# Streaming attention and a wave layer on one core: the order of all steps from a list schedule, and the values of both head parities in one two-bank tile

## The chip, the cores and the metric

The kernel runs on one core of a Trainium2 chip. TensorE (PE) multiplies matrices and writes to PSUM, VectorE (DVE), ScalarE (ACT) and GpSimd (POOL) do the rest, and transfers are issued from the queues of SyncE (SP) and POOL. Each engine takes its instructions in the order in which the program wrote them. The metric is device time in microseconds of one execution, as the median of several runs.

## The reference, cut to what matters

```python
# q, k, v: 4 batches x 8 heads x 768 positions x 64; heads 0, 2 and 6 are "retrieval"
scores = scale * np.matmul(q, k.transpose(0, 1, 3, 2))
stream_keep = causal & (is_sink | in_win)      # 4 sink keys, or a window of 64
mask = np.where(retr, causal, stream_keep)
a = softmax(np.where(mask, scores, -1e9))
x = np.matmul(a, v)                            # heads side by side: 4 x 768 x 512
theta = x @ w_theta
zr, zi = x * np.cos(theta), x * np.sin(theta)
y = w_tok_r @ zr + w_tok_i @ zi                # over the 768 positions
u = x + y
return u + np.maximum(u @ w_ch, 0.0)
```

## The kernel before, in words

Heads are taken in four pairs, n = 0 to 3, and positions in blocks of 128. For each batch b the steps are these. `transposes(b, n)` turns q and k of a pair (PE, line 151) and copies them out of PSUM (ACT line 155, DVE line 157). `score_unit` multiplies keys by queries (line 215) into a two-bank tile `ps`, ACT takes the exponential (lines 231 to 243), and DVE multiplies a causal triangle (lines 253, 256) or the window mask (line 224) in; there are 14 such units a batch and one for the sink keys (line 283). `cast_v` makes bf16 values `vt` and a copy `vx` shifted by half a block. `values(b, i)` multiplies probabilities by values for one block i (line 312), first for the even heads and then for the odd, each in a one-bank tile `pav`; DVE takes a reciprocal (line 314) and multiplies (line 316). `turn_x` turns x, `phases` multiplies by w_theta (line 333), ACT takes cosine and sine (lines 338, 339), DVE makes zr (line 341) and POOL zi (line 342). `mix` multiplies by the two token weights (line 372), adds x (line 376), turns u (line 353), multiplies by w_ch (line 360), makes the output tile `ot` (line 362) and stores it. Token weights are turned on the chip too (line 393). Three pools hold PSUM: `ps_s` has two tiles of two banks (scores, phases), `ps_m` two of one bank (mix, channel) and `ps_x` two of one bank (all transposes and `pav`).

The order is what the program writes. Generators yield at places with an estimated cost in ns, and `weave` always continues the one that is least far along its given total; it runs attention of batch b + 1 beside `mix` of batch b. Within attention, the order is a list written by hand. The first batch stands ahead of this, written out:

```python
    weave((scores(high_all, 7, 1), 6300), (early(0), 5500))
```

The transfers of weights and of the next q and k are issued from POOL's queue at places in the same text; v and the output go through SP's queue.

Of the kernel before, what the change touches and what calls it, by code (L numbers as in the profile page):

```python
# [9 lines left out]
F32 = mybir.dt.float32  # L10
# [11 lines left out]
def drain(gen):  # L22
    for _ in gen:
        pass


def weave(*parts):

    live = [[0.0, n, g, float(total)] for n, (g, total) in enumerate(parts)]
    while live:  # L30
        live.sort(key=lambda x: (x[0] / x[3], x[1]))
        part = live[0]
        try:
            part[0] += next(part[2])
        except StopIteration:
            live.pop(0)
# [3 lines left out]
def kernel(  # L40
# [17 lines left out]
    NB = S // 128  # L58
    KD = DM // 128
# [19 lines left out]
    m_causal = const.tile([128, 128], BF16, name="m_causal")  # L79
# [9 lines left out]
    kS = [big.tile([128, 128], BF16, name=f"kS{n}") for n in range(4)]  # L89
# [8 lines left out]
    NQ = S // 64  # L98
    P_st = big.tile([128, len(STREAM), NQ * 128 + 64], BF16, name="P_st")

    state = {}


    def load_v(b, pairs=range(4), after=None):
        src = v[b].rearrange("h (j p) d -> p h j d", p=128)
        for n in pairs:
            t = stage.tile([128, 2, NB, D], F32, tag="st_v", name="st_v")
            state["v", b, n] = t
            if after is not None:

                nc.vector.tensor_copy(t[:, :, 0, 0], after[:, :2])
            for x, h in enumerate(PAIRS[n]):
                nc.sync.dma_start(out=t[:, x], in_=src[:, h])


    def load_qk(b, heads=slice(0, 8)):
        for what, a in (("q", q), ("k", k)):
            if (what, b) not in state:
                state[what, b] = two.tile([128, H, NB * D], BF16, tag=f"{what}b", name=f"{what}b")
            src = a[b].rearrange("h (p j) d -> p h (j d)", p=128)  # L120
            nc.gpsimd.dma_start(out=state[what, b][:, heads], in_=src[:, heads])

    def cast_v(b, n, first=False):
        t = state["v", b, n]
        h0, h1 = PAIRS[n]
        (nc.vector if first else nc.gpsimd).tensor_copy(vt[:, h0:h1 + 1:2, :, :D], t)  # L126
        for x, h in enumerate((h0, h1)):
            if not IS_RETR[h]:
                s = STREAM.index(h)
                if first:  # L130
                    nc.vector.tensor_copy(vx[:64, s], vt[:64, h])  # L131
                    nc.vector.tensor_copy(vx[64:, s, 1:], vt[64:, h, :NB - 1])
                else:
                    nc.gpsimd.tensor_copy(vx[:64, s, :, :D], t[:64, x])
                    nc.gpsimd.tensor_copy(vx[64:, s, 1:, :D], t[64:, x, :NB - 1])

    def sinks(n):
# [7 lines left out]
    def transposes(b, n):  # L145
        h0, h1 = PAIRS[n]
        for what, dst in (("q", qT), ("k", kT)):
            pt = ps_x.tile([128, 1024], BF16, tag="x", name="pt")
            for j in range(NB):
                for x, h in enumerate((h0, h1)):  # L150
                    nc.tensor.transpose(pt[64 * x:64 * x + 64, j * 128:(j + 1) * 128], state[what, b][:, h, j * D:(j + 1) * D], ident)  # L151
            o = dst[n].rearrange("d (p j) -> d p j", j=NB)
            i = pt[:, :S].rearrange("d (j p) -> d p j", j=NB)
            if (what == "q" and n < 2) or (b > 0 and (what == "q" or n < 2)):
                nc.scalar.copy(o, i)  # L155
            else:
                nc.vector.tensor_copy(o, i)
        sinks(n)
# [16 lines left out]
    pending = []  # L175

    def masks_now():
        while pending:
            pending.pop(0)()

    def score_unit(n, banks, un):
        ps = ps_s.tile([128, 2, 512], F32, tag="s", name="ps")
# [3 lines left out]
        if used:  # L186
            P = big.tile([128, sum(used)], BF16, tag=f"P{un}", name=f"P{un}")
        masks = []
        for y, (x, h, what) in enumerate(banks):
            rows = slice(64 * x, 64 * x + 64)  # L190
            if isinstance(what, list):
                c = 0
                for j, q0, w in what:
                    mms[y].append((ps[:, y, c:c + w], kT[n][rows, j * 128:(j + 1) * 128], qT[n][rows, q0:q0 + w]))
                    for i in range(q0 // 128, (q0 + w) // 128):
                        at = y * used[0] + c + i * 128 - q0
                        state["P", h, j, i] = P[:, at:at + 128]
                        if i == j:
                            masks.append(at)
                    c += w  # L200
                width.append(c)
            else:
                q0, w = what
                for c in range(NQ):
                    lo = max(64 * c if c != 1 else 0, q0)
                    hi = min(64 * c + 128, S, q0 + w)
                    if lo < hi:
                        half = slice(64 * (c % 2), 64 * (c % 2) + 64)
                        mms[y].append((ps[half, y, lo - q0:hi - q0], kT[n][rows, c * 64:(c + 1) * 64], qT[n][rows, lo:hi]))
                width.append(w)  # L210
        for m in range(max(map(len, mms))):
            for y in range(2):
                if m < len(mms[y]):
                    o, l, r = mms[y][m]
                    nc.tensor.matmul(o, l, r, start=True, stop=True, skip_group_check=True)  # L215
# [6 lines left out]
        def stream_mask(o, q0, w, heads):  # L222
            m = m_stream[:, q0:q0 + w].rearrange("p (c x) -> p c x", x=64).unsqueeze(1).to_broadcast([128, heads, w // 64, 64])
            nc.vector.tensor_tensor(o, o, m, ALU.mult)

        lists = [isinstance(what, list) for _, _, what in banks]
        w0, w1 = width
        if not any(lists):
            q0, w = banks[0][2]
            o = stream_out(banks[0][1], 2, q0, w)  # L230
            nc.scalar.activation(o, ps[:, :, :w].rearrange("p s (c x) -> p s c x", x=64), AF.Exp, scale=scale)  # L231
            pending.append(lambda: stream_mask(o, q0, w, 2))
        elif all(lists):
            if w0 == w1:
                nc.scalar.activation(P.rearrange("p (y c) -> p y c", y=2), ps[:, :, :w0], AF.Exp, scale=scale)  # L235
            else:
                assert w0 == 512
                nc.scalar.activation(P, ps.rearrange("p y c -> p (y c)")[:, :512 + w1], AF.Exp, scale=scale)
        else:
            nc.scalar.activation(P, ps[:, 0, :w0], AF.Exp, scale=scale)  # L240
            q0, w = banks[1][2]
            o = stream_out(banks[1][1], 1, q0, w)
            nc.scalar.activation(o[:, 0], ps[:, 1, :w].rearrange("p (c x) -> p c x", x=64), AF.Exp, scale=scale)
            pending.append(lambda: stream_mask(o, q0, w, 1))

        def causal():
            todo = list(masks)
            while todo:
                at = todo.pop(0)
                if len(set(used)) == 1 and at + used[0] in todo:  # L250
# [330 lines left out]
```

## Time and profile before

| | |
|---|---|
| median of 3 runs | 257.67 us (254.26 to 260.39) |
| the profiled execution | 255.57 us, of which the span is 253.9 us |
| busy: PE, DVE, ACT, POOL | 196.1, 141.2, 115.8, 81.9 us |

The span is the time from the first to the last instruction; an execution's own time has 1.7 us more around it. A busy PE includes the modelled end of each matmul, so it isn't a PE at its peak; what counts is where PE sits idle, and until when.

### The profile page before, as it was taken

To read this page: it belongs to the slowest core of one execution; us is meant where nothing else is said; L and a number is where in the kernel's file an instruction comes from. 1 tells how busy PE (TensorE), PEld (TensorE's weight loads), DVE (VectorE), ACT (ScalarE), POOL (GpSimd) and SP (SyncE) were. 2 spreads that over 40 slices of the span, in tenths; PEclk is the share of its full clock that TensorE was granted. 3 is DMA by queue.
4 is the path that set the end of the run, shared out by engine and by line. 5 is a ranking of instruction groups with operands and counts; after the bars stand their busy time and mean duration, and the time that the engine had idled before them with its cause. 6 is when DMAs were issued, how large, how long until landed. Compare 5 with 4: busy or idle time off the path is not lost.

```text
span 253.9 us, 5096 instructions
## 1 busy us (share of the span) xinstructions
PE 196.1 (77%) x2124; PEld 111.2 (44%) x2124; DVE 141.2 (56%) x318; ACT 115.8 (46%) x150; POOL 81.9 (32%) x121
## 2 busy tenths in 40 slices
PE   1585004978668998896969999986699999959992
PEld 0452002765245455564424556543245665424440
DVE  6665106665824656763469477625584776572442
ACT  2435001544548892226698633355887332711110
POOL 8805000001952960003099700044593000650000
PEclk9999999999999999999999999999999999999998
DMA  5999990820056089901205597101100111021113
GB/s 77 179 198 218 193 205 10 186 65 3 0 96 114 5 182 180 235 28 41 85 1 125 112 196 153 41 3 60 65 3 0 44 45 41 0 83 44 50 74 124
DMA packets 39758, 22.62 MB, mean 89 GB/s; under 512 B 25912, under 2 KB 36664, under 8 KB 39736
## 3 DMA queue, kind: packets, MB, share of 16 engines
q0 software_dynamic: 11072, 9.70, 24.7%
q1 hardware_dynamic: 28664, 12.61, 19.2%
q8 instruction: 16, 0.26, 0.4%
q14 instruction: 6, 0.05, 0.1%
HBM read 25.71 MB, written 6.29 MB: 126 GB/s over the span
## 4 chain that ended last, share of the span: by engine, by line
PE 53%; ACT 14%; DMA 13%; DVE 8%; issue 5%; POOL 4%; SPq 1%; POOLq 0%; DVEq 0%; ACTq 0%
PE py L372 20%; DMA st_v<-in_v_dram 9%; PE pav L312 8%; PE ps L333 6%; PE pc L360 6%; PE ps L215 6%; ACT P L235 3%; DMA qb<-in_q_dram 3%; POOL zi L342 3%; ACT qT L155 3%; ACT st L339 2%; DVE ot L362 2%; ACT ct L338 2%; PE pt L151 2%; PE pt L353 2%
## 5 line engine op out<-in xcount | busy, mean ns | idle before, releaser
L342 POOL TENSOR_TENSOR zi<-x,st 128x512 bf16<-128x512 bf16 x24 | 30.9, 1306 | 123.0 <-ACT st L339 122.7
L372 PE MATMUL py<-zr,wtokTr 128*128 128x512 bf16 x144 | 39.4, 380 | 2.5 <-DVE zr L341 2.5
L372 PE MATMUL py<-zi,wtokTi 128*128 128x512 bf16 x144 | 39.2, 379 | 0.4 <-POOL zi L342 0.4
L235 ACT ACTIVATE P<-ps 128x1024 bf16<-128x1024 f32 (+2 forms) x24 | 21.1, 917 | 24.9 <-PE ps L215 24.9
L341 DVE TENSOR_TENSOR zr<-x,ct 128x512 bf16<-128x512 bf16 x24 | 20.9, 910 | 17.1 <-ACT ct L338 17.1
L215 PE MATMUL ps<-qT,kT 64*64 64x128 bf16 (+6 forms) x380 | 26.3, 263 | 5.1 <-ACT P L235 4.7
L312 PE MATMUL pav<-vx,P_st 128*128 128x65 bf16 x120 | 17.0, 201 | 16.4 <-DVE vx L131 16.4
L355 ACT COPY uT<-pt 128x512 bf16<-128x512 bf16 x24 | 14.2, 593 | 33.7 <-PE pt L353 33.7
L376 DVE TENSOR_TENSOR u<-x,py 128x512 bf16<-128x512 bf16 x24 | 16.5, 686 | 21.0 <-PE py L372 20.7
L360 PE MATMUL pc<-w_ch_sb,uT 128*128 128x512 bf16 x96 | 24.6, 380 | 2.8 <-DVE ot L362 2.8
L338 ACT ACTIVATE ct<-ps,half_pi 128x1024 f32<-128x1024 f32 x12 | 13.4, 1117 | 28.2 <-PE ps L333 27.2
L333 PE MATMUL ps<-w_theta_sb,xT 128*128 128x512 bf16 x96 | 23.3, 379 | 0.0
L312 PEld LDWEIGHTS <-P_st 128*128 128x128 bf16 x240 | 14.1, 103 | 20.7 <-issue 19.5
L362 DVE SCALAR_TENSOR_TENSOR ot<-pc,u 128x512 f32<-128x512 f32 x24 | 16.5, 689 | 11.5 <-PE pc L360 8.9
L215 PEld LDWEIGHTS <-kT 64*64 64x64 bf16 (+1 forms) x380 | 12.7, 111 | 20.5 <-issue 18.2
L316 DVE TENSOR_TENSOR x<-pav,r 128x256 bf16<-128x256 f32 x48 | 20.4, 424 | 1.7
L372 PEld LDWEIGHTS <-wtokTi 128*128 128x128 bf16 x144 | 13.0, 98 | 14.9 <-issue 3.3
L312 PE MATMUL pav<-vt,P 128*128 128x65 bf16 x252 | 15.6, 203 | 3.7 <-DVE vt L126 1.7
L231 ACT ACTIVATE P_st<-ps 128x1024 bf16<-128x1024 f32 (+1 forms) x16 | 12.9, 814 | 10.2 <-PE ps L215 10.2
L314 DVE RECIPROCAL r<-pav 128x4 f32<-128x4 f32 x48 | 8.6, 179 | 15.6 <-PE pav L312 15.0
L312 PE MATMUL pav<-vt,P_st 128*128 128x65 bf16 x120 | 17.2, 202 | 0.0
L372 PEld LDWEIGHTS <-wtokTr 128*128 128x128 bf16 x144 | 12.0, 97 | 11.8 <-issue 1.7
(75 smaller groups left out, 320.2 us busy)
## 6 DMA issues: line engine op xcount, KB each, us to landing
st_v<-in_v_dram SPq DMA_DIRECT2D x32, 192.0 KB
out_dram<-ot SPq DMA_DIRECT2D x24, 256.0 KB
qb<-in_q_dram POOLq DMA_DIRECT2D x3, 768.0 KB, 10.5
kb<-in_k_dram POOLq DMA_DIRECT2D x3, 768.0 KB, 14.6
wtok<-in_moe_w_tok_r_dram POOLq DMA_DIRECT2D x3, 384.0 KB, 10.2
wtok<-in_moe_w_tok_i_dram POOLq DMA_DIRECT2D x3, 384.0 KB, 11.8
w_theta_sb<-in_moe_w_theta_dram POOLq DMA_DIRECT2D x1, 512.0 KB, 11.0
w_ch_sb<-in_moe_w_ch_dram POOLq DMA_DIRECT2D x1, 512.0 KB, 8.6
```

The lines of the kernel that those rows point to most:

```text
L215: nc.tensor.matmul(o, l, r, start=True, stop=True, skip_group_check=True)
L235: nc.scalar.activation(P.rearrange("p (y c) -> p y c", y=2), ps[:, :, :w0], AF.Exp, scale=scale)
L312: nc.tensor.matmul(o, l, r, start=(m == 0), stop=True, skip_group_check=True)
L316: nc.vector.tensor_tensor(dst, av[:, :, :D], r.unsqueeze(2).to_broadcast([128, 4, D]), ALU.mult)
L333: nc.tensor.matmul(ps[:, y], xT[:, kk, (i + y) * 128:(i + y + 1) * 128], w_theta_sb[:, kk], start=(kk == 0), stop=(kk == KD - 1))
L338: nc.scalar.activation(ct, ps, AF.Sin, bias=half_pi)
L341: nc.vector.tensor_tensor(state["zr", b][:, i + y], x[:, i + y], ct[:, y], ALU.mult)
L342: nc.gpsimd.tensor_tensor(state["zi", b][:, i + y], x[:, i + y], st[:, y], ALU.mult)
L360: nc.tensor.matmul(pc, uT[t][:, kk], w_ch_sb[:, kk], start=(kk == 0), stop=(kk == KD - 1))
L362: nc.vector.scalar_tensor_tensor(ot, pc, 0.0, u[t], ALU.max, ALU.add)
L372: nc.tensor.matmul(py, w[:, s, t * 128:(t + 1) * 128], z[:, s], start=(n == 0), stop=(n == len(order) - 1))
L376: nc.vector.tensor_tensor(u[t], x[:, t], py, ALU.add)
```

## The change

All work becomes `Step`s with an engine, a duration in ns, the steps that must come first, a PSUM or SBUF slot that it takes and steps whose slots it gives back. `Plan.order` runs a list schedule over them: whenever an engine is free it takes the ready step with the longest remaining path, with penalties for a switch of TensorE's tile shape or of ACT's table, and the steps are then emitted in the order of their planned starts. The transfers are steps of a made-up engine "DMA", one after another. The weights' transfers get a `hold`: they are planned behind the cast of the third pair of v.

Beside the order, the change does these things. One two-bank tile from `ps_s` holds the values of both parities, with one reciprocal and one multiplication. The causal triangles move from DVE to POOL, as selects in place. The shifted copies `vx` of batch 0 and some clearing move from DVE to POOL, four of the six zi of batch 0 from POOL to DVE, and batch 0's copies of turned x from DVE to ACT. All 14 score units of batch 0 come ahead of its values.

```diff
+    LATENCY = {"PE": (230, 0), "ACT": (190, 60), "DVE": (120, 60), "POOL": (150, 60), "SP": (50, 0), "DMA": (2000, 0)}
+    SWITCH = {"PE": 95, "ACT": 1300}
+    HOLD = {"PE": 1500, "ACT": 8000}
...
+                    value = -ready_at[id(s)] if e == "DMA" else rank[id(s)] + s.bias
+                    if s.mode and s.mode != mode.get(e):
+                        value -= self.HOLD.get(e, 0)
...
+        out.sort(key=lambda s: s.start)
...
+    plan = Plan({"s": 2, "m": 2, "x": 2, "u": 4, "uT": 3, "ot": 2, "ct": 2, "st": 2, "wtok": 4, "st_v": 4})
...
-                    nc.vector.tensor_tensor(blk, blk, m_causal.unsqueeze(1).to_broadcast([128, 2, 128]), ALU.mult)
...
+                    sel(blk, -1, [[0, 2], [1, 128]], 0)
...
+    def values(b, i):
+        pav = ps_s.tile([128, 2, 512], F32, tag="s", name="pav")
+        state["av", b, i] = av = pav[:, :, :4 * (D + 1)].rearrange("p t (g c) -> p t g c", c=D + 1)
...
+    def normalize(b, i):
+        av = state.pop(("av", b, i))
+        r = work.tile([128, 2, 4], F32, tag="r", name="r")
+        nc.vector.reciprocal(r, av[:, :, :, D])
+        dst = state["x", b][:, i].rearrange("p (g t d) -> p t g d", t=2, d=D)
+        nc.vector.tensor_tensor(dst, av[:, :, :, :D], r.unsqueeze(3).to_broadcast([128, 2, 4, D]), ALU.mult)
...
+                eng = "DVE" if b == 0 and i else "POOL"
...
+    hold = [cast[0, 2]]
+    issue = add("POOL", 780, lambda: nc.gpsimd.dma_start(out=w_theta_sb, in_=moe_w_theta.rearrange("(ko ki) n -> ki ko n", ki=128)), hold)
...
+    for s in order:
+        if s.fn is not None:
+            s.fn()
```

POOL's queue at the start, before: behind the masks of the window, up to the first zi. `kS` are the sink keys, `wtok` the token weights, `qb` and `kb` q and k of batch 1.

```order
L421 DMA w_theta_sb<-in_moe_w_theta_dram 128x4x512
L418 AFFINE_SELECT m_stream<-m_stream 64x6x64 x2
...
L400 DMA wtok<-in_moe_w_tok_r_dram 128x2x768
L400 DMA wtok<-in_moe_w_tok_i_dram 128x2x768
...
L121 DMA qb<-in_q_dram 128x8x384
L121 DMA kb<-in_k_dram 128x8x384
L400 DMA wtok<-in_moe_w_tok_r_dram 128x2x768
L400 DMA wtok<-in_moe_w_tok_i_dram 128x2x768
L342 TENSOR_TENSOR zi<-x,st 128x512 x6
```

The same queue now, from the first shifted copy, which reads the second pair of v.

```order
L228 COPY vx<-vt 64x390
L229 COPY vx<-vt 64x325
L240 COPY kS_98<-kT_95 64x4 x2
L200 AFFINE_SELECT P_235<-P_235 128x2x128 x2
L674 DMA w_theta_sb<-in_moe_w_theta_dram 128x4x512
...
L487 DMA wtok<-in_moe_w_tok_r_dram 128x2x768
...
L487 DMA wtok<-in_moe_w_tok_i_dram 128x2x768
...
L200 AFFINE_SELECT P_430<-P_430 128x2x128
L208 DMA qb<-in_q_dram 128x8x384
L208 DMA kb<-in_k_dram 128x8x384
L487 DMA wtok<-in_moe_w_tok_r_dram 128x2x768
```

All the large transfers have moved behind work that reads v; ahead of it stand the triangles and the sink keys.

ACT between attention of batches 2 and 3, before: cosine `ct` and sine `st`, copies of the next q and k, and the first exponential.

```order
L338 ACT_TABLE_LOAD
L338 ACTIVATE ct<-ps,half_pi 128x1024
L339 ACTIVATE st<-ps 128x1024
L155 COPY qT_89<-pt 128x768
L155 COPY kT_93<-pt 128x768
L355 COPY uT<-pt 128x512
L155 COPY qT_90<-pt 128x768
L155 COPY kT_94<-pt 128x768
...
L155 COPY qT_92<-pt 128x768
L235 ACT_TABLE_LOAD
L235 ACTIVATE P_2564<-ps 128x1024
```

ACT at the same place now, behind the load of the table.

```order
L437 ACTIVATE ct<-ps,half_pi 128x1024 x2
L439 ACTIVATE st<-ps 128x1024 x2
L437 ACTIVATE ct<-ps,half_pi 128x1024
L439 ACTIVATE st<-ps 128x1024
L258 COPY qT_89<-pt 128x768
...
L258 COPY qT_88<-pt 128x768
L338 ACT_TABLE_LOAD
L338 ACTIVATE P_st<-ps 128x2x8x64
L468 COPY uT<-pt 128x512
L258 COPY kT_92<-pt 128x768
```

The sines now stand together ahead of the copies, and the first pair's k is copied behind the first exponential, which is of a window unit.

## Rows read from the trace of the kernel before

**Rows 1.** The page: busy time of each engine, then PE in 40 slices (tenths).

```profile
PE 196.1 (77%) x2124; PEld 111.2 (44%) x2124; DVE 141.2 (56%) x318; ACT 115.8 (46%) x150; POOL 81.9 (32%) x121
...
PE   1585004978668998896969999986699999959992
```

**Rows 2.** Busy time by stretch: PE, PEld, DVE, ACT, POOL, then clock, DMA share, GB/s.

```profile
0.00:26.00 26.00, 13.25 (x163) 8.50 (x164) 16.44 (x41) 10.74 (x13) 14.77 (x33) 1.00 1.07 169
26.00:42.30 16.30, 1.20 (x11) 0.69 (x9) 3.20 (x11) 0.00 (x0) 0.00 (x0) 1.00 0.90 151
42.30:63.00 20.70, 18.00 (x234) 12.64 (x233) 13.17 (x43) 9.53 (x13) 0.45 (x1) 1.00 0.35 78
63.00:80.25 17.25, 12.45 (x148) 7.11 (x148) 8.60 (x10) 9.85 (x14) 10.81 (x12) 1.00 0.46 77
80.25:130.00 49.75, 44.13 (x536) 25.32 (x534) 30.07 (x70) 29.77 (x40) 17.12 (x25) 1.00 0.48 97
130.00:181.20 51.20, 45.12 (x515) 25.11 (x515) 31.03 (x70) 28.35 (x37) 19.82 (x29) 1.00 0.44 94
181.20:226.40 45.20, 39.34 (x408) 21.60 (x406) 29.74 (x66) 24.09 (x31) 18.88 (x24) 1.00 0.05 20
226.40:253.90 27.50, 22.61 (x121) 10.18 (x118) 8.96 (x13) 3.52 (x6) 0.00 (x0) 0.96 0.22 84
```

**Rows 3.** The timeline from 0 to 48 us: start, duration, instruction, idle time before it.

```profile
9.66 21.49 SPq L113 DMA_DIRECT2D st_v<-in_v_dram  x8
...
14.17 0.85 PE L151 MATMUL pt<-ident,kb 128*64 128x128 bf16 x12 [1.05 <-DMA kb<-in_k_dram]
...
37.63 0.56 DVE L126 CAST vt<-st_v 128x768 bf16<-128x768 f32 x1 [11.52 <-DMA st_v<-in_v_dram]
...
40.66 0.56 DVE L126 CAST vt<-st_v 128x768 bf16<-128x768 f32 x1 [1.36 <-DMA st_v<-in_v_dram]
```

**Rows 4.** DMA from 14.2 to 26 us, by queue: packets, MB, share of 16 engines.

```profile
q0 software_dynamic: 1674, 1.69, 87.1%
q1 hardware_dynamic: 3101, 0.78, 34.4%
```

**Rows 5.** DMA from 45 to 52.4 us, when no other load ran.

```profile
q1 hardware_dynamic: 5903, 1.48, 88.8%
```

**Rows 6.** Three of PE's longest idle times in batches 2 and 3.

```profile
174.54 0.38 PE L353 MATMUL pt<-ident,u 128*128 128x128 bf16 x4 [2.02 <-ACT qT L155]
...
183.57 0.28 PE L215 MATMUL ps<-qT,kT 64*128 64x256 bf16 x2 [1.66 <-ACT P L235]
...
225.39 1.02 PE L360 MATMUL pc<-w_ch_sb,uT 128*128 128x512 bf16 x4 [2.85 <-DVE ot L362]
```

**Rows 7.** Groups by line and shape: count, busy us, mean ns, idle before.

```profile
L316 DVE TENSOR_TENSOR x<-pav,r 128x256 bf16<-128x256 f32 x48 | 20.4, 424 | 1.7
L376 DVE TENSOR_TENSOR u<-x,py 128x512 bf16<-128x512 bf16 x24 | 16.5, 686 | 21.0 <-PE py L372 20.7
L314 DVE RECIPROCAL r<-pav 128x4 f32<-128x4 f32 x48 | 8.6, 179 | 15.6 <-PE pav L312 15.0
L134 POOL CAST vx<-st_v 64x384 bf16<-64x384 f32 x15 | 8.9, 592 | 0.3
L400 POOL DMA_DIRECT2D wtok<-in_moe_w_tok_r_dram x3 | 2.2, 733 | 0.0
L418 POOL TENSOR_SCALAR_AFFINE_SELECT m_causal<-m_causal 128x128 bf16<-128x128 bf16 x1 | 0.3, 340 | 0.0
```

**Rows 8.** The page, parts 3 and 5: POOL's queue over the whole span; all score multiplications.

```profile
q0 software_dynamic: 11072, 9.70, 24.7%
...
L215 PE MATMUL ps<-qT,kT 64*64 64x128 bf16 (+6 forms) x380 | 26.3, 263 | 5.1 <-ACT P L235 4.7
```

**Rows 9.** Transposes of one q tile once 55 us are past.

```profile
71.91 0.53 PE L151 MATMUL pt<-ident,qb 128*64 128x128 bf16 x12
```

**Rows 10.** One line's instructions: min, median and max ns, first and last start.

```profile
L253 DVE TENSOR_TENSOR P<-P,m_causal x24: 280/292/936, 12.0 to 199.4; 128x256 bf16<-128x256 bf16 x24
```

More of the change, by code (lines that the diff above doesn't have):

```diff
@@ L19, with __init__ @@
 STREAM = [1, 3, 5, 7, 4]
[L22 to L36, printed above, removed]
+class Step:
+    def __init__(self, eng, ns, fn, after, take, give, mode, bias):
+        self.eng, self.ns, self.fn, self.after = eng, ns, fn, [a for a in after if a is not None]
+        self.take, self.give, self.mode, self.bias = take, list(give), mode, bias
+        self.users = 0
+        self.start = self.end = None
@@ L87 @@
     kT = [big.tile([128, S], BF16, name=f"kT{n}") for n in range(4)]
-    kS = [big.tile([128, 128], BF16, name=f"kS{n}") for n in range(4)]
+    kS = [None] + [big.tile([128, 128], BF16, name=f"kS{n}") for n in (1, 2, 3)]
     vt = big.tile([128, H, NB, D + 1], BF16, name="vt")
@@ L116, in load_qk @@
[L116 to L124, printed above, removed]
-        h0, h1 = PAIRS[n]
[L126 to L135, printed above, removed]
@@ L173, in units, with score_steps @@
         return [(n, [(0, h0, w), (1, h1, w)])]
[L175 to L182, printed above, removed]
+    def score_steps(b, un, n, banks, after, before_exp):
+        gives = {}
         mms = [[], []]
@@ new lines, with weights @@
+    gate[1].after.append(gate[0])
+    gate[2].after.append(gate[1])
+    turned, kept, sinkk, scored, sunk, cast, shift = {}, {}, {}, {}, {}, {}, {}
+    av, norm, xt, xk, th, zs, ud, ch = {}, {}, {}, {}, {}, {}, {}, {}
+    weight = {}
+    last_pool = []
+    def weights(t, c, after):
+        for n in range(2):
+            issue = add("POOL", 750, lambda n=n, t=t: fetch_wtok(n, t, c), after + last_pool, take="wtok")
+            last_pool[:] = [issue]
+            land = add("DMA", 2600, None, [issue])
+            steps = []
+            for y in range(c):
+                tw = add("PE", 336, lambda n=n, t=t + y: turn_w(n, t), [land], take="x", mode="128")
+                steps.append(tw)
+                weight[n, t + y] = add("DVE" if n else "ACT", 557 if n else 720, lambda n=n, t=t + y: keep_w(n, t), [tw], give=[tw])
+            for tw in steps:
+                tw.give.append(issue)
+                issue.users += 1
@@ new lines, with load_steps @@
+    turn_steps(0)
+    v_steps(0)
+    hold = [cast[0, 2]]
+    issue = add("POOL", 780, lambda: nc.gpsimd.dma_start(out=w_theta_sb, in_=moe_w_theta.rearrange("(ko ki) n -> ki ko n", ki=128)), hold)
+    last_pool[:] = [issue]
+    theta_w = add("DMA", 3300, None, [issue])
+    weights(0, 2, [])
+    def load_steps(b, after):
+        for what in "qk":
+            issue = add("POOL", 900, lambda what=what, b=b: load_qk(what, b, slice(0, 8)), after + last_pool, bias=-20000)
+            last_pool[:] = [issue]
+            land = add("DMA", 5000, None, [issue])
+            for n in range(4):
+                landed[what, b, n] = land
@@ new lines @@
+    load_steps(1, [])
+    weights(2, 2, [])
+    issue = add("POOL", 780, lambda: nc.gpsimd.dma_start(out=w_ch_sb, in_=moe_w_ch.rearrange("(ko ki) n -> ki ko n", ki=128)), last_pool)
+    last_pool[:] = [issue]
+    channel_w = add("DMA", 3300, None, [issue])
+    weights(4, 2, [])
+    ones_done = add("POOL", 600, sink_ones, [cleared[3]])
+    sink_done = []
+    for half in range(2):
+        first = add("SP", 500, lambda half=half: sink_values(2 * half), [cleared[2]] + sink_done)
+        land = add("DMA", 100, None, [first])
+        sink_done.append(add("DVE", 480, lambda half=half: nc.vector.tensor_copy(vs[:32, 2 * half:2 * half + 2, :, :D], vs_f), [land, cleared[3], ones_done]))
@@ L549 @@
+    attention_steps(0)
+    for b in range(1, B):
+        turn_steps(b)
+        v_steps(b)
+        if b + 1 < B:
+            load_steps(b + 1, [kept[what, b - 1, n] for what in "qk" for n in range(4)])
+        attention_steps(b)
+        mlp_steps(b - 1)
+    mlp_steps(B - 1)
+    order = plan.order({"PE": 0, "ACT": 2100, "DVE": 2500, "POOL": 9000})
+    state["order"] = order
+    PLANS.append(plan)
+    for s in order:
+        if s.fn is not None:
+            s.fn()
+PLANS = []
 _INS = ['q', 'k', 'v', 'is_retrieval', 'n_sink', 'window', 'moe_w_theta', 'moe_w_tok_r', 'moe_w_tok_i', 'moe_w_ch']
```

653 lines of the change are left out of this document (374 added, 279 removed).

## The prediction

> **What bounds the kernel now.** The page comes first: PE is busy for 196.1 of 253.9 us and no other engine for more than 56% [rows 1]. So the question is where PE's 57.8 idle us lie. The slices answer roughly: an almost empty stretch at 26 to 38 us, then nines with a dip or two in each later batch. The stretches say it exactly [rows 2]: 12.8 us of idle time up to 26 us and 15.1 from there to 42.3, then 2.7 and 4.8 up to 80.25, then 5.6, 6.1 and 5.9 in the three stretches in which attention of one batch runs beside the mixing of another, and 4.9 in the tail. About half of all idle time lies ahead of the first values.
>
> The timeline names what ends it [rows 3]. q and k of batch 0 are there at 14.2 us, where the last k tile is turned. Then everything waits for v: its eight loads sit in SP's queue from 9.7 to 31.2 us, the third pair is cast at 37.6 and the fourth at 40.7. Why so late is seen in the DMA rows. From 14.2 to 26 us POOL's queue moves 1.69 MB (w_theta, token weights, then q and k of batch 1) while v gets 3101 of its packets through [rows 4], 263 a us. Batch 1's v, with no other queue in use, moves 5903 packets in 88.8% of 7.4 us [rows 5], 898 a us. In the later batches PE waits for ACT's copies out of `ps_x` (2.02 us), for an exponential behind the load of ACT's table (1.66 us) and for an `ot` on DVE behind zr (2.85 us) [rows 6].
>
> **The start.** All large transfers move behind the third pair of v in POOL's queue. v is 8 loads of 768 packets; at 898 a us that is 6.8 us, so it lands at about 21 us. If it got no more than 263 a us, it would take 23.4 us and land at 37.6, as now: these are the two ends. I take the first, since from 14.2 to some 20 us no other load is left in a queue.
>
> What is late next is POOL. It makes the five shifted copies, each of two instructions of about 0.59 us [rows 7], so 5.9 us against the quarter of a us that each took on DVE; among them stand three issues of 0.73 us, so 2.2. The first copy needs the second pair, landed at about 17.6 (half of 6.8 us) and cast by 18.2. Two sink keys and two selects of up to 0.68 us (twice the 0.34 of one block [rows 7]) add about 1.3 us. That gives 18.2 + 5.9 + 2.2 + 1.3 = 27.6 us for the last copy, so for the first values; the last landing, its cast and two copies alone would give 24. ACT is no later: its 14 exponentials at some 0.8 us (13 of its instructions took 10.74 us by 26 us [rows 2]) and a few copies fit in from 9 us on. I take 27.6 instead of 42.3, a gain of 14.7 us.
>
> Six of the 14 units now stand ahead of the values, inside the wait. PE spends 26.3 us on 56 units [rows 8], 0.47 each, more at the start, where 12 transposes take 0.85 us at 14.2 us [rows 3] against 0.53 at 71.9 [rows 9]: the array runs at the lower of its two levels (1.2 GHz) first and rises somewhere between. (The clock column reads 1.00 in all these stretches, so I go by the durations.) Six units are 2.8 to 4.5 us; 3.5 leave the path.
>
> From 42.3 to 80.25 PE idles for 7.5 us, the larger part in front of the first mix, where six zi follow each other on POOL. Four of them go to DVE. But POOL's own loads come later now: w_theta, two token weights, q and k of batch 1 are 2.9 MB (0.52 + 2 x 0.39 + 2 x 0.79), and that queue needs 24.7% of 253.9 us for 9.70 MB [rows 8], 6.5 us a MB, so 18.7 us. Issued from some 21.5 us on, they end at 40, or at 47 if v of batch 1 (SP's queue issues it as soon as its buffers are free) takes its 6.8 us out of theirs; the next token weights need 5 more. PE asks for those some 17 us after the first values, at 45. So a wait of 0 to 7 us comes back, and I count 1.3 us gained here, not 5. Together the start gains 14.7 + 3.5 + 1.3 = 19.5 us.
>
> **The batches.** The same matmuls run, so PE's work stays. The 17.6 idle us of the three stretches are what another order can win. The sines now stand together ahead of the copies of q and k, zr and zi come sooner, and the first exponential waits for one window unit; the last phases of batch 3 are covered by three channel products of batch 2. Against it, each two-bank tile of values sits in `ps_s`, which scores and phases need too, until DVE has normalised it. That costs one reciprocal (0.18) and one multiplication of 512 columns, about the 0.69 us of u, which also reads PSUM, in place of 2 x (0.18 + 0.42) = 1.20 us [rows 7]. At 0.9 us a block and two tiles, DVE keeps pace with PE. DVE also loses the triangles and 24 x 0.3 = 7 us of normalising, but DVE isn't late now, so that earns nothing by itself. Bounds: 15 us gained if all but a us a stretch goes, 3 us lost if the tiles in `ps_s` cost each stretch another us. I take 8 us, nearest to the rows that name waits which the new order removes (2.02 + 1.66 + 2.85 and their like).
>
> The triangles cost POOL 12 selects a batch: six of one block at 0.34 us and six of two blocks at 0.34 to 0.68 [rows 7], 4.1 to 6.1 us. POOL was busy for 17 to 20 of 50 us there [rows 2], so it has room. Cover ends where a select stands ahead of the values that need it. What DVE and POOL do to each other is seen in the triangles now: median 292 ns, longest 936 [rows 10], beside POOL's casts. The Trainium skill speaks against this move: "SBUF — State Buffer", section "SBUF: two separate sides", says that the two engines share a port pair as an exclusive lock for a whole instruction and the loser fully blocks, where DVE has two SBUF inputs and POOL reads SBUF. The 936 ns agree. By the row's median the selects cost nothing on the path; by the rule they come back as a rival below.
>
> **The sum.** 255.57 - 19.5 - 8 = 228.1 us for the profiled execution. The median is 2.1 us above it, so **230 us**.
>
> **Rivals.** *The order takes nearly all the idle time*: 24 us at the start (values at 24 us) and 15 in the batches, 255.6 - 39 + 2.1 = 219. For it: PE's work of 196 plus the unavoidable first 5 and last 5 us is 206. Against: no engine's durations are as steady as a plan's. *Only the start gains*: 238; the two tiles of `ps_s` or a plan that misjudges ACT give back what the order wins. *Masks and casts block each other*: if half of 12 selects a batch put 0.64 us (936 - 292 ns) each on the path, in three batches, that is 12 us: 242. This is what the rule of "SBUF — State Buffer" would do. *v lands no sooner*, held by SP's own issues, which took 21.5 us for eight while other loads ran [rows 3]: then only the units and the batches gain, 255.6 - 8 + 2.1, about 249. Against it: alone, seven loads were issued and moved in 7.4 us [rows 5]. *The array stays at the lower level*: it rose late in the run before, and if the new order's small gaps keep it low, each of 120 matmuls of 512 columns a batch costs twice its 0.21 us (four take 1.02 with the modelled end of the last [rows 6]), 25 us a batch. Low until the end of batch 1 gives 230 + 25 plus some 7 us for values and transposes, 262; from there on it is slower than before. Against it: at 71.9 us transposes run at the upper level though PE idled for 4.8 of the 17 us around them [rows 2].
>
> **Chances.** Forecast 0.58, all idle time 0.13, start only 0.13, blocking 0.07, v no sooner 0.04, low clock 0.05. The likeliest gives 230. The range of 218 to 243 takes in the first four. A run's scatter makes 2% (about 5 us) the least that can be told from no change: faster 0.91 (the first four), same 0.05, slower 0.04.
>
> **What would show it.** In the new profile: the fourth cast of v at 21 to 23 us, not 40.7; first values at 25 to 29 us; POOL's issue of w_theta behind the third cast; the first exponential of batch 1 at about 60, not 81 us; a wait of PE on a token weight's DMA at 44 to 50 us; PE idle for 2 to 4 us in each of the three stretches; no triangle on DVE, and selects of 0.34 to 0.7 us on POOL. I am wrong if v is still cast near 38 us, if selects take over 1 us with values waiting behind them, or if transposes still take 0.85 us in the middle of the run.

## Result and the profile after

The kernel after takes **229.2 us** (median of 4 runs, 228.2 to 229.7) against 256.7 us before: a ratio of 0.895 (95% interval 0.887 to 0.904). The prediction was 230. The profiled execution takes 229.25 us with a span of 227.5. Runs of the kernel before spread from 254.3 to 262.2 us and those of e1 below from 240.3 to 246.9; the ratios leave out the slower ones and two single runs (before at 639 us, e8 at 374), and e1's profile is of a run of 246.5 us.

The page of after: busy times, PE in 40 slices, then the granted clock in tenths.

```profile
PE 195.2 (86%) x2124; PEld 113.1 (50%) x2124; DVE 122.2 (54%) x203; ACT 120.2 (53%) x156; POOL 101.1 (44%) x180
...
PE   0688549968997899999999999959999999689990
...
PEclk9999999999999589999999999997999999999997
```

PE's busy time is that of [rows 1] within a us, so nearly all of the 26.4 us of span are idle time that went: 57.8 before, 32.3 now. The empty slices at 26 to 38 us are gone; a 5 and a 4, between 22.8 and 34.1 us, are what is left of them. New are the dips in the clock row: [rows 2] read 1.00 up to the tail.

ACT loads its table once a batch ahead of the first exponential (of batch 1 at 80.25 us before, 64.60 now), so these loads cut both runs into similar stretches: [rows 2] ends its own at 80.25, 130.0 and 181.2. After's, busy time of PE, PEld, DVE, ACT and POOL, clock, DMA share, GB/s:

```profile
0.00:64.60 64.60, 46.04 (x570) 31.13 (x572) 35.78 (x61) 32.48 (x42) 37.68 (x78) 1.00 1.01 166
64.60:112.60 48.00, 44.62 (x536) 27.02 (x533) 24.73 (x44) 30.00 (x39) 24.77 (x42) 0.93 0.55 114
112.60:160.74 48.14, 45.43 (x515) 25.02 (x514) 27.24 (x44) 28.94 (x38) 21.45 (x36) 0.96 0.24 67
160.74:227.50 66.76, 59.08 (x513) 29.95 (x511) 34.45 (x54) 28.80 (x38) 17.20 (x26) 0.98 0.13 48
```

The start is shorter by 80.25 - 64.60 = 15.65 us, the three other stretches by 1.75, 3.06 and 5.94 us (before: 49.75, 51.20 and 72.70, the last two of [rows 2] together). So by these cuts the start gave 15.65 and the batches 10.75 us. PE idles for 3.4, 2.7 and 7.7 us in the later three.

The first cut is not at the same place of the work, though: 36 multiplications by token weights stand ahead of it in after and 22 before. PE's idle time shows the split without that work: ahead of the first cut it fell from 35.4 to 18.6 us, by 16.8, and in the other stretches by 2.2, 3.4 and 3.1, together 8.7; PE's own work took the remaining 0.9 us less.

The timeline of after in the start (start, duration, instruction, idle time before it and what ended it):

```profile
8.61 10.18 SPq L218 DMA_DIRECT2D st_v<-in_v_dram  x8
19.31 0.96 DVE L260 COPY qT<-pt 128x768 bf16<-128x768 bf16 x1 [1.53 <-PE pt L251]
20.18 0.55 DVE L222 CAST vt<-st_v 128x768 bf16<-128x768 f32 x1
20.80 0.50 POOL L228 COPY vx<-vt 64x390 bf16<-64x390 bf16 x1 [1.50 <-DVE vt L222]
23.93 0.76 POOL L674 DMA_DIRECT2D w_theta_sb<-in_moe_w_theta_dram  x1
26.30 0.54 DVE L222 CAST vt<-st_v 128x768 bf16<-128x768 f32 x1
30.72 0.21 PE L409 MATMUL pav<-vx,P_st 128*128 128x65 bf16 x1 [0.79 <-POOL vx L228]
33.19 0.51 DVE L698 CAST vs<-vs_f 32x640 bf16<-32x640 f32 x1 [5.18 <-DMA vs_f<-in_v_dram]
34.60 0.52 PE L409 MATMUL pav<-vt,P 128*128 128x65 bf16 x6 [1.80 <-DVE x L416]
65.90 1.02 ACT L338 ACTIVATE P_st<-ps 128x1024 bf16<-128x1024 f32 x1
```

v's eight loads are issued in 10.2 us instead of the 21.5 of [rows 3], and the first of its casts stands at 20.18, the fourth at 26.30 instead of 40.66. But the first cast didn't wait for v any more: it follows a copy of q on DVE, and that waited for PE. DMA rows say the same: from 14.7 to 20.5 us, with no other queue in use, v moves at 716 packets a us (263 in [rows 4]), and from 20.5 to 24 us v's queue moves 33 packets in all.

```profile
q1 hardware_dynamic: 4153, 1.04, 79.6%
...
q1 hardware_dynamic: 33, 0.01, 1.0%
```

The groups by line and shape (count, busy us, mean ns, idle before) that answer to [rows 7]:

```profile
L442 DVE TENSOR_TENSOR zr<-x,ct 128x512 bf16<-128x512 bf16 x24 | 27.9, 1197 | 1.3 <-ACT ct L437 1.3
L416 DVE TENSOR_TENSOR x<-pav,r 128x512 bf16<-128x512 f32 x24 | 16.6, 691 | 0.8
L200 POOL TENSOR_SCALAR_AFFINE_SELECT P<-P 128x256 bf16<-128x256 bf16 x24 | 10.0, 435 | 5.8 <-ACT P L341 5.4
L200 POOL TENSOR_SCALAR_AFFINE_SELECT P<-P 128x128 bf16<-128x128 bf16 x24 | 6.5, 294 | 11.5 <-ACT P L346 6.6 <-ACT P L344 4.7
L455 PE MATMUL py<-zr,wtokTr 128*128 128x512 bf16 x144 | 39.7, 385 | 6.3 <-DVE zr L442 6.3
```

Normalising (0.69) and the selects (0.29 and 0.44) cost what was said. What stands out is zr: 1197 ns in the mean, and 6.3 us of PE's waiting behind it, the largest entry after the first 6.5 us for q and k. The lines by themselves (ns, least, median and longest; start of the first and the last), zr of before first, and the place in batch 2 of after:

```profile
L341 DVE TENSOR_TENSOR zr<-x,ct x24: 678/693/1644, 61.5 to 223.1; 128x512 bf16<-128x512 bf16 x24
...
L442 DVE TENSOR_TENSOR zr<-x,ct x24: 676/1045/3587, 46.8 to 201.1; 128x512 bf16<-128x512 bf16 x24
...
L445 POOL TENSOR_TENSOR zi<-x,st x20: 1155/1604/1614, 49.4 to 202.2; 128x512 bf16<-128x512 bf16 x20
```

```profile
147.35 8.55 POOL L445 TENSOR_TENSOR zi<-x,st 128x512 bf16<-128x512 bf16 x6 [0.43 <-ACT st L439]
147.98 4.21 DVE L442 TENSOR_TENSOR zr<-x,ct 128x512 bf16<-128x512 bf16 x3
150.68 0.38 PE L455 MATMUL py<-zr,wtokTr 128*128 128x512 bf16 x1 [1.27 <-DVE zr L442]
152.24 2.38 PE L455 MATMUL py<-zr,wtokTr 128*128 128x512 bf16 x7 [1.19 <-DVE zr L442]
```

### The profile page after: what moved, and what is told of

It is laid out like the page before. It is cut to its first block, busy times and chain, and to the rows that moved or that the text cites. A ratio compares the mean times of both kernels' runs of the same rounds, so it can differ in the third digit from the quotient of the medians.

```text
span 227.5 us, 5040 instructions
## 1 busy us (share of the span) xinstructions
PE 195.2 (86%) x2124; PEld 113.1 (50%) x2124; DVE 122.2 (54%) x203; ACT 120.2 (53%) x156; POOL 101.1 (44%) x180
## 3 DMA queue, kind: packets, MB, share of 16 engines
q0 software_dynamic: 11072, 9.70, 27.4%
## 4 chain that ended last, share of the span: by engine, by line
PE 72%; DVE 8%; ACT 6%; DMA 5%; POOL 3%; issue 3%; POOLq 1%; SPq 1%; DVEq 0%; ACTq 0%
PE py L455 26%; PE pav L409 9%; PE ps L322 9%; PE pc L474 7%; PE pt L251 7%; PE ps L432 6%; DVE zr L442 5%; POOL zi L445 3%; PE pt L421 3%; PE pt L464 3%; DMA vs_f<-in_v_dram 2%; PE pt L494 2%; DMA kb<-in_k_dram 2%; ACT P L341 2%; ACT P_st L338 1%
## 5 line engine op out<-in xcount | busy, mean ns | idle before, releaser
L445 POOL TENSOR_TENSOR zi<-x,st 128x512 bf16<-128x512 bf16 x20 | 27.8, 1421 | 25.2 <-ACT st L439 19.8
L455 PE MATMUL py<-zi,wtokTi 128*128 128x512 bf16 x144 | 38.5, 379 | 0.1
L459 DVE TENSOR_TENSOR u<-x,py 128x512 bf16<-128x512 bf16 x24 | 16.5, 687 | 36.1 <-PE py L455 36.1
L442 DVE TENSOR_TENSOR zr<-x,ct 128x512 bf16<-128x512 bf16 x24 | 27.9, 1197 | 1.3 <-ACT ct L437 1.3
L468 ACT COPY uT<-pt 128x512 bf16<-128x512 bf16 x24 | 13.9, 586 | 26.5 <-PE pt L464 26.4
L478 DVE SCALAR_TENSOR_TENSOR ot<-pc,u 128x512 f32<-128x512 f32 x24 | 16.5, 688 | 16.4 <-PE pc L474 15.1
L222 POOL CAST vt<-st_v 128x768 bf16<-128x768 f32 x12 | 10.2, 856 | 33.3 <-DMA st_v<-in_v_dram 33.1
L322 PEld LDWEIGHTS <-kT 64*64 64x64 bf16 (+1 forms) x380 | 13.6, 113 | 21.7 <-issue 17.1
L200 POOL TENSOR_SCALAR_AFFINE_SELECT P<-P 128x256 bf16<-128x256 bf16 (+1 forms) x48 | 16.5, 365 | 17.2 <-ACT P L346 6.6
L474 PE MATMUL pc<-w_ch_sb,uT 128*128 128x512 bf16 x96 | 24.0, 380 | 0.0
L437 ACT ACTIVATE ct<-ps,half_pi 128x1024 f32<-128x1024 f32 x12 | 13.0, 1113 | 20.1 <-PE ps L432 19.5
L455 PEld LDWEIGHTS <-wtokTr 128*128 128x128 bf16 x144 | 12.6, 98 | 19.7 <-issue 7.6
L258 ACT COPY qT<-pt 128x768 bf16<-128x768 bf16 x14 | 11.0, 802 | 18.7 <-PE pt L251 18.5
L358 DVE TENSOR_TENSOR P_st<-P_st,m_stream 128x512 bf16<-128x512 bf16 (+2 forms) x24 | 12.8, 543 | 14.7 <-ACT P_st L349 10.5
L409 PE MATMUL pav<-vt,P 128*128 128x65 bf16 x252 | 16.1, 207 | 1.8 <-DVE x L416 1.8
```

What stands on the lines that cost most here:

```text
L200: nc.gpsimd.affine_select(out=t, in_=t, compare_op=ALU.is_ge, fill=0.0, base=base, pattern=pattern, channel_multiplier=cm)
L322: nc.tensor.matmul(ps[half, yy, c:c + w], l, r, start=True, stop=True, skip_group_check=True)
L409: nc.tensor.matmul(o, l, r, start=(m == 0), stop=True, skip_group_check=True)
L442: nc.vector.tensor_tensor(state["zr", b][:, i + y], state["x", b][:, i + y], state["ct", b, i][:, y], ALU.mult)
L445: (nc.vector if eng == "DVE" else nc.gpsimd).tensor_tensor(state["zi", b][:, i + y], state["x", b][:, i + y], state["st", b, i][:, y], ALU ...
L455: nc.tensor.matmul(py, wtokT[n][:, s, t * 128:(t + 1) * 128], z[:, s], start=(g == 0 and m == 0), stop=(g == 2 and m == 3))
```

## Experiments

"First table load" is ACT's load ahead of batch 1's first exponential in the profiled run, and "rest" what is left of the span. "PE idle" is PE's idle time ahead of that load and behind it; it is left out where added work fills it (e10, e11) and where 27 to 29 of PE's 2124 records are missing (e1 to e4). Runs e1 to e4 are of one chip, e5 to e8 of a second, e9 to e12 of a third.

| kernel | median us | ratio to before (95%) | first table load | rest | PE idle |
|---|---|---|---|---|---|
| before | 254.3 to 262.2 | | 80.25 | 173.65 | 35.4, 22.5 |
| after | 229.2 | 0.895 (0.887 to 0.904) | 64.60 | 162.90 | 18.6, 13.8 |
| e1 | 246.6 (240.3 to 246.9) | | 65.30 | | |
| e2 | 237.8 | 0.931 (0.924 to 0.938) | 71.67 | 164.33 | |
| e3 | 224.7 | 0.880 (0.870 to 0.890) | 61.34 | 160.16 | |
| e4 | 226.3 | 0.886 (0.883 to 0.890) | 60.85 | 163.95 | |
| e5 | 229.6 | 0.892 (0.881 to 0.903) | 63.45 | 164.15 | 18.6, 13.6 |
| e6 | 231.5 | 0.901 (0.891 to 0.912) | 64.77 | 164.63 | 14.6, 15.5 |
| e7 | 255.0 | 0.981 (0.965 to 0.996) | 78.31 | 172.19 | 34.0, 21.9 |
| e8 | 224.6 | 0.870 (0.854 to 0.885) | 60.03 | 162.97 | 16.5, 13.8 |
| e9 | 223.5 | 0.873 (0.868 to 0.879) | 61.48 | 160.42 | 16.1, 12.3 |
| e10 | 228.4 (223.2 to 229.2) | | 63.12 | 164.38 | |
| e11 | 225.1 | 0.881 (0.874 to 0.889) | 62.05 | 160.35 | |
| e12 | 223.2 | 0.873 (0.867 to 0.878) | 60.96 | 160.24 | 15.2, 12.0 |

**e1: the late loads alone, in the old order.** Theory: v landing early is half of the gain whatever the order. Rival: it is the order that gains.

```diff
-    nc.gpsimd.dma_start(out=w_theta_sb, in_=moe_w_theta...)
-    fetch_wtok(0, 2)
...
         cast_v(0, n, True)
+    nc.gpsimd.tensor_copy(w_theta_sb[:, 0, :2], vt[:, PAIRS[2][1], 0, :2])
+    nc.gpsimd.dma_start(out=w_theta_sb, in_=moe_w_theta...)
+    fetch_wtok(0, 2)
```

> The kernel before with one edit: w_theta and the token weights are issued from POOL behind a small copy that reads the third pair of v, so the loads of w_theta, token weights, q and k of batch 1 all leave after v has landed. Theory (half of the gain is v landing early, whatever the order is): v lands at 20 to 22 us, the first values come at about 25 instead of 42.3, the missing weights give back up to 5 us near 45 us, so 12 to 17 us less than before, 240 to 245. Rival (it is the order of the steps that gains, the loads only let it): within 5 us of before, 252 to 257, since what was idle at 26 to 42 comes back as a wait for the late token weights or for the next q and k.

The fastest run takes 240.3 us, 14.7 less than the three fastest of before beside it (254.7, 255.0 and 255.4), as the theory said. The profile, of another run, has the fourth cast at 25.36 us, and batch 1's exponentials begin 15 us sooner, nearly as soon as in the kernel after:

```profile
25.36 0.63 DVE L126 CAST vt<-st_v 128x768 bf16<-128x768 f32 x1
...
65.30 1.28 ACT L235 ACT_TABLE_LOAD   x1
```

**e2: the new order without the late loads.** The five issues of w_theta, two token weights, q and k of batch 1 come first on POOL; all else stays in its order.

```diff
+    ahead = [early]
...
-    state["order"] = order
+    state["order"] = order = ahead + [p for p in order if p not in ahead]
```

> The kernel after with the same order of all steps on PE, ACT and DVE, but w_theta, the first two token weights and q and k of batch 1 are issued first on POOL, ahead of all else there. Theory: v is held back as before, lands at 31 to 37 us, the first values are complete at 38 to 42 instead of 30.8; the weights come sooner, so the net loss is 6 to 11 us: 235 to 241. Rival (transfers move the start little because POOL's shifted copies bound it): under 232.

237.8 us, 8.6 above the kernel after, and 7.1 of them ahead of the first table load. The eight loads of v sit in SP's queue for 24.5 us again, and DVE waits 6.8 us for a cast:

```profile
8.51 24.52 SPq L218 DMA_DIRECT2D st_v<-in_v_dram  x8
...
32.01 0.56 DVE L222 CAST vt<-st_v 128x768 bf16<-128x768 f32 x1 [6.80 <-DMA st_v<-in_v_dram]
...
36.80 0.54 DVE L222 CAST vt<-st_v 128x768 bf16<-128x768 f32 x1
```

So both theories hold a part: late loads alone win 15.0 us of the start, the new order alone 8.6, both together 15.65. By PE's idle time ahead of the first table load it is some 14, 7 and 16.8 us (a few records are missing in e1 and e2): the overlap is smaller there, but not gone. They win in part the same idle time: an order that fills the wait for v with score units leaves less of it to be won. A second reason is in the rows: in e1 DVE makes the shifted copies and is done with them at 27.4 us, where POOL's last ends at 31.2 in the kernel after.

**e3: zi off POOL.** All zi of batches 1 to 3 on DVE, each at its planned place.

```diff
-                zs[b, "i", i + y] = add(..., lambda b=b, i=i, y=y, eng=eng: z_imag(b, i, y, eng), ...)
+                zs[b, "i", i + y] = add(..., lambda b=b, i=i, y=y, eng=eng: z_imag(b, i, y, "DVE" if b else eng), ...)
```

> The kernel after, its order kept; only the engine of the zi of batches 1 to 3 changes from POOL to DVE, each at its planned place. Theory (zr on DVE takes 1.64 us instead of 0.69 wherever a zi runs on POOL, and PE's waits at 150.7, 152.2, 198.1 and 199.7 us follow from that): zr back to 0.69 us, those four waits of 1.2 us go, and so does the fall of the granted clock at 153 us: 4 to 7 us less, 222 to 225. Rival (DVE becomes late with 18 more instructions of 0.69 us, 12 us): no change or up to 4 us slower, 229 to 233.

224.7 us; the rest behind the first table load is 2.7 us shorter than in the kernel after and 4.0 shorter than in e5, so the theory holds at its lower end (what is more in the median lies in the start, e5). The intervals of the two ratios overlap; the times themselves don't (223.2 to 225.7 against 227.7 to 231.0 of after and e5). zr's line and the same place of batch 2:

```profile
L442 DVE TENSOR_TENSOR zr<-x,ct x24: 676/681/3583, 43.6 to 195.4; 128x512 bf16<-128x512 bf16 x24
```

```profile
147.08 1.67 PE L455 MATMUL py<-zr,wtokTr 128*128 128x512 bf16 x7 [0.68 <-DVE zr L442]
```

The median zr takes 681 ns instead of 1045; the longest is one of batch 0, where two zi are still on POOL. PE's two waits of 1.27 and 1.19 us have become one of 0.68 (and one of 0.62 for a zi at 151.8), and the seven multiplications take 1.67 us where they took 2.38: the clock didn't fall here.

**e4: the triangles back on DVE.** PE's and ACT's order kept.

```diff
-                    sel(blk, -1, [[0, 2], [1, 128]], 0)
+                    nc.vector.tensor_tensor(blk, blk, m_causal..., ALU.mult)
...
```

> The kernel after with PE's and ACT's order kept; the 48 causal selects on POOL become multiplications by a triangle on DVE again, at their planned places. Theory (as predicted, the selects have cover): within 2 us of the kernel after, 227 to 231, a little faster at most from POOL being free sooner for the shifted copies of batch 0. Rival (selects and DVE's work block each other): 3 us or more faster, below 226.

226.3 us, some 3 less than the kernel after and between the two theories. But the rest is 163.95 us, as in after (162.9) and e5 (164.15); the difference lies ahead of the first table load, where e3, which changes nothing there, shows the same, and e5 says why. So the selects earn and cost nothing that can be told.

**e5: the kernel after again**, on the chip of e6 to e8.

> The kernel after, unchanged, on the chip on which the next three run. The two kernels e3 and e4 began batch 0's sines 3.1 to 3.3 us sooner than the first profile of after, though nothing ahead of that differs; their clock rows show a stretch of 3.4 us at the upper level at 12 us and the lasting rise at 33 to 36 instead of 40.4 us. If that is chance of the run or the chip and not the edits, the kernel after gives 225 to 229 us here, with the sines at 41 to 44 us; if it is the edits, 228 to 230.

229.6 us (227.7 to 231.0), with the table of the sines loaded at 42.8 us. So the median doesn't change, but the start of one and the same program does: its first table load stands at 64.60 and 63.45 us in the two profiles of after, and at 61.34 in e3, which changes nothing ahead of that. What differs is when the array rises to its upper level for good: at 40.4 us in after, 37.8 in e5, 36.0 in e3 and 33.0 in e4, and the first table loads follow in that order (64.60, 63.45, 61.34, 60.85). PE's idle time ahead of them is nearly the same, 18.4 to 18.8 us in all four (a few records are missing in e3 and e4). So e3's and e4's sooner start is PE's work taking less time, and no wait that went; after wasn't run on their chip, so whether the chip has a part in it stays open. In e3's profile the array was also at the upper level for a while early on, where transposes at 15.06 took 0.85 us in after:

```profile
14.50 0.53 PE L251 MATMUL pt<-ident,qb 128*64 128x128 bf16 x12
```

Gains in the first column of the table are believed here only beyond 3 us.

**e6: values in one-bank tiles again**, each parity with its own reciprocal and multiplication, order from the schedule.

```diff
-        pav = ps_s.tile([128, 2, 512], F32, tag="s", name="pav")
+        pav = ps_x.tile([128, 512], F32, tag="x", name="pav")
```

> The kernel after with the values of each head parity in a one-bank tile of their own in the pool of the transposes, as before, each with its reciprocal and its multiplication, the order from the same schedule. Theory (the order wins, the tile does little): within 3 us of the kernel after, DVE busy 7 us more. Rival (two tiles of one pool for values and all transposes were the bound in the batches): 4 us or more above the kernel after, 232 to 238.

231.5 us, 2 above e5 on the same chip, within the theory's 3 and with intervals that overlap; the rest is 164.6. PE doesn't wait longer for it: it idles for 30.1 us in all, 32.2 in e5. It is busy longer, 199.4 us against 195.4, with the clock at 0.5 from 67.7 to 84.7 us, in e5 only from 72.0 to 78.8. **e7** makes the opposite edit to the kernel before.

> The kernel before with one edit: the values of both parities in one two-bank tile of the scores' pool, with one reciprocal and one multiplication; order as written by hand. Theory: 253 to 259, no change that can be told, or 1 to 4 us slower, as the scores then wait for tiles. Rival (the tile by itself carries the gain in the batches): 245 to 251.

255.0 us, a ratio of 0.981: the two fastest runs (251.9 and 252.4) are some 3 us below the fastest of before beside them (255.3), and in the profile the rest is 1.5 us shorter. Not the rival, but not nothing: the tile may be worth 2 to 3 us in either order, which is too near the scatter to be sure of.

**e8: the start's two waits.** The shifted copies of batch 0 on DVE, and the second cast of sink values behind batch 0's last turned x.

```diff
+    shift[b, h] = add("POOL" if b else "DVE", 960 if b else 500, ...)
...
     attention_steps(0)
+    sinks_of(1, sink_done + [xk[0, 5]])
```

> The kernel after with two edits at the start: the shifted copies of batch 0 are made by DVE (planned there at 0.5 us a pair), and the second cast of the sink values, for which DVE waited 5.2 us ahead of the first normalisation, is planned behind batch 0's last turned x. Theory (POOL's copies hold the first values from 27 to 30.7 us and the cast holds the third block to 34.6): first values complete at 27 to 28, no wait of PE behind the normalisation, 3 to 5 us less than the kernel after. Rival (the late weights or DVE take it back): within 1 us of it.

224.6 us, 5 less than e5 on the same chip, with intervals that overlap slightly. The first values are complete at 28.5 us instead of 30.7 (31.7 in e5), and the wait behind the normalisation is gone. The profile puts 3.4 of the 5 us ahead of the first table load, which is hardly more than the start varies by itself: 2.1 of them are idle time (18.6 to 16.5), the others PE's work, with the array at the upper level from 32.8 us here and from 37.8 in e5. So some 2 us are the edit's; whether more is stays open.

**e9: both gains together**, with all 24 zi on DVE.

> The two edits of e8_start_dve and, in the same order, all 24 zi on DVE (e3_zi_dve_same_order had moved those of batches 1 to 3). Theory (the two gains lie at different places, 4.7 us each against the kernel after): 218 to 222 us, PE's waits on zr down to under 2.5 us in all. Rival (DVE, now with zi and the shifted copies, becomes late and gives one of them back): 223 to 226.

223.5 us: the rival's figure, 1.2 less than e3 with intervals that overlap. The 6.3 us of waits on zr are down to 1.2, but two waits of 2.7 and 2.6 us stand in the start that the kernel after doesn't have and e8 has too: a window mask behind the five shifted copies on DVE, and phases that wait for ACT's sine.

```profile
29.55 0.23 PE L409 MATMUL pav<-vx,P_st 128*128 128x65 bf16 x1 [2.72 <-DVE P_st L358]
...
44.53 1.82 PE L432 MATMUL ps<-w_theta_sb,xT 128*128 128x512 bf16 x4 [2.62 <-ACT st L439]
```

Behind the first table load e9 is 2.6 us shorter than e8 (162.97 to 160.42), and PE idles 1.5 us less there: zi on DVE is worth this much beside e8's edits.

**e12: three of the five shifted copies back on POOL.**

```diff
+    here = b == 0 and n == 3
+    shift[b, h] = add("DVE" if here else "POOL", 700 if here else 960, ...)
```

> The kernel of e9_start_and_zi, but of the five shifted copies of batch 0 only the two of the fourth pair are made by DVE (planned at 0.7 us), three by POOL as in the kernel after. In e9 PE waited 2.7 us at 29.6 us for a window mask that stood behind the five copies on DVE. Theory (work shared between the two engines lands the first values sooner): this wait under 1.5 us, first values complete at 27 to 28.5 us, 221 to 223 us. Rival (POOL's issues of loads hold its three copies, so the last of them is as late): 223 to 225.

The first values are complete at 28.4 us and the wait for the mask is gone, two of 0.9 and 0.5 us are left, and the time is the same as e9's: 223.2 us. This is the fastest kernel here, 6.0 us below after, with intervals apart. PE idles 5.2 us less than in after, 3.4 of them ahead of the first table load and 1.8 behind it, so the edits of the start carry the larger part of it and zi on DVE the smaller. The wait for the sine is left in the start.

**e10 and e11: does PE's clock bound the start?** e10 puts 11 multiplications of ones into the wait for the first q and k; e11 adds the same to e9, and three more ahead of every score unit and of four blocks of values.

```diff
+    for _ in range(11):
+        nc.tensor.matmul(idle, ones[:, :128], ones, start=True, stop=True)
```

> The kernel after with 11 matmuls of 512 columns of ones, whose result nothing reads, while PE waits for the first q and k; nothing else changes. They add work on PE and take none away. Theory (the array's rise to its upper level follows what PE has done, and it ran at the lower level up to 36 to 40 us because PE was idle for most of the first 6 us and had gaps later): the first transposes take 0.53 instead of 0.85 us, batch 0's sines come 1 to 4 us sooner, 225 to 228 us. Rival (the rise depends on the gaps after 6 us alone, or the first stretch is bound by DMA and ACT): no change, 228 to 230.

Three of four runs give 228.1 to 229.2 us, as the kernel after and as the rival said; one gave 223.2 and has no profile, so what it did stays open. In the profiled run the array is at the upper level for the second pair's k and falls within the next transposes:

```profile
10.30 0.53 PE L251 MATMUL pt<-ident,kb 128*64 128x128 bf16 x12 [1.19 <-DMA kb<-in_k_dram]
10.66 0.81 PE L251 MATMUL pt<-ident,qb 128*64 128x128 bf16 x12
...
15.28 0.85 PE L251 MATMUL pt<-ident,qb 128*64 128x128 bf16 x12
```

> The kernel of e9_start_and_zi with the 11 matmuls of ones of e10_idle_matmuls ahead of the first transposes and three more ahead of each of the 14 score units and of the first four blocks of values of batch 0: 54 more matmuls that take no work away, 11.6 us of PE at the upper level, 23 at the lower. Theory (in e10 the array rose at 7.3 us and fell at 10.7 because of PE's idle time between 8 and 10.3 us): it stays at the upper level through the start, transposes take 0.53 us at 15 to 20 us, and what the fillers cost lies in PE's waits: 218 to 224 us. Rival (the fall has another cause, or the fillers stand on the path): the transposes still take 0.85 us, 226 to 236.

```profile
15.16 0.50 PE L251 MATMUL pt<-ident,kb 128*64 128x128 bf16 x12
```

```profile
4.80:45.70 40.90, 34.63 (x458) 19.16 (x457) 23.68 (x49) 22.82 (x30) 19.02 (x43) 1.00 1.10 190
...
14.80:25.00 10.20, 10.20 (x143) 4.86 (x139) 6.10 (x9) 6.81 (x10) 3.96 (x13) 1.00 0.78 174
```

With the gaps filled the array keeps the upper level from 4.8 to 45.7 us, so the theory on the fall holds. It gains nothing: 225.1 us against 223.5, where the theory said 218 to 224; the fillers themselves keep PE busy without a break from 14.8 to 25 us, as the second row shows. With fewer fillers it wasn't tried.

## Why the prediction was right, and where its steps were off

**The whole.** 228.1 was said for the profiled execution and 229.25 came. The sum was made in PE's idle time, and so measured the start was put at 19.5 us and gave 16.8, the batches were put at 8 and gave 8.7, and PE's work, put at no change, took 0.9 less. By the table loads it is 15.65 and 10.75. Either way the start gave less than was said and the rest more, so that the total is this close is in part luck. The 2.1 us by which the median was put above the profiled execution didn't come either (229.2 against 229.25).

**Start: v.** Right: it lands at 20.5 us (21 said), because nothing else is in a queue; e2 takes that away and DVE waits for v again. The fourth cast at "21 to 23" was wrong, though: it stands at 26.3 by DVE's order, behind masks and the sink values; the copies that read it came later still on POOL.

**Start: the first values.** This is the term that was mis-sized: "14.7 us", values at 27.6; it measured 11.5, values at 30.8. POOL was named rightly as what is late next. Its row of copies, issues, sink keys and selects took 10.4 us (20.80 to 31.18, of which the first values didn't wait for the last 0.5) where 9.4 was worked out; the larger part of the error is where it begins, 20.8 instead of 18.2, since the step let the cast follow the landing of v at once and left out what DVE has ahead of that cast (a copy of q that waits for PE, whose 12 transposes take 0.85 us there). e8 and e12, with copies on DVE, have the values at 28.5 and 28.4.

**Start: units and weights.** 3.5 + 1.3 us were said for what follows the values; 15.65 - 11.5 = 4.15 came, 5.3 by idle time (16.8 - 11.5). Batch 1's first exponential stands at 65.9, not 60. The wait on a token weight did not come back: the second pair of them landed at 50.2 and 52.7 us, near the end of what was worked out (45 to 52), but PE turns the first of it at 57.3 us, not 45. The landing of batch 1's q and k, 42.5 and 47.9, was close to the 40 to 47 worked out.

**Batches.** 8 us were said, as nearest to the waits named in [rows 6]; 8.7 us of idle time went, inside the bounds of 15 gained and 3 lost. Those three waits are gone, and PE idles for 3.4 and 2.7 us in the first two stretches, where 2 to 4 were said. Behind the first table load PE idles for 22.5 us before, 21.9 with the tile alone (e7), 15.5 with the new order and the old tile (e6) and 13.8 in after, and the triangles earn nothing that can be told (e4). So the order must carry the larger part, with the smaller moves that no run took back; no run changed the order behind the start by itself.

**The rival of blocking.** It was set at the selects, and there it was wrong: e4. But what it describes happens at zr: 0.68 us alone, 1.64 beside a zi on POOL, which itself takes 1.61 instead of 1.16. They wait for each other in turn: in batch 2 a zi of 148.47 ends at 150.08 us, the zr started beside it at 148.98 ends 0.55 us later, and the next zi, started at 150.04, ends 1.02 us behind that zr. The longest zr (3.59 us, in batch 0) began beside an issue on POOL that two zi followed, and ended 0.55 us behind the second. The Trainium skill says this in "SBUF — State Buffer", section "SBUF: two separate sides" (the shared port pair is held for a whole instruction, and the other engine blocks); the trace agrees. e3, and e9 beside e8, put its price at 2.6 to 4 us, in which the second fall of the clock (below) is included. The order before met it too (zr up to 1.64 us in batches 0 and 3), but started most of its zr alone: 7 of 24 took over 1 us, 14 in the new order, which brings the sines together and with them zr and zi.

**The rival of the low clock.** It came in small: two falls of 10.2 us in all, with transposes of 0.85 us again at 154.55 (last section).

## What to carry to other kernels

When two edits fill the same idle time, price each with the other in place: here 15 and 8.6 us made 15.65. Before two profiles are cut at the same instruction and compared, count what work stands ahead of the cut in each. Before bringing VectorE's and GpSimd's work closer together, ask which instructions of the two will now run side by side, since an order made from durations measured alone doesn't know that they get longer. The first result after the long wait was set here by the engine that handles the data last, and by what stood ahead of it there, not by the landing: look for both.

## What the runs showed of the hardware

The granted clock falls to 0.5 in the kernel after at places where PE had short waits. Stretches of after, the clock being the third number from the end:

```profile
72.40:74.50 2.10, 1.12 (x10) 0.50 (x10) 0.40 (x1) 2.10 (x3) 2.02 (x5) 1.00 0.98 113
74.60:81.30 6.70, 5.95 (x74) 4.54 (x73) 2.47 (x7) 5.03 (x9) 1.63 (x5) 0.50 1.27 198
81.50:88.00 6.50, 6.12 (x132) 4.71 (x128) 4.59 (x11) 3.71 (x4) 0.00 (x0) 1.00 0.11 33
153.10:156.40 3.30, 3.05 (x31) 1.76 (x31) 3.30 (x3) 0.96 (x2) 3.30 (x4) 0.50 0.00 0
```

At 0.5 the array is at 1.2 GHz: multiplications of 512 columns follow each other by 0.43 us (e10's first, from 1.92 us on) instead of 0.215 (seven in 1.67 us in e3, the last with its modelled end). Ahead of the first fall PE waited three times for exponentials, 0.3 to 0.7 us each, and was busy for 1.12 of 2.10 us; ahead of the second stand the two waits on zr. The second fall is in the profiled run of every kernel that keeps after's order and its zi on POOL (after, e2, e4, e5, e8, e10) and in none with zi on DVE (e3, e9, e11, e12); the first is in all ten, and e2, e4, e5 and e10 have a third one in batch 3. The two of after last 10.2 us and cost at most half of that; what the first costs by itself was not measured. The clock row of after reads 1.00 ahead of 40.4 us, yet 12 transposes take 0.85 us there (0.53 later), so that row is to be checked against durations.
